# A local-attention and gated-FFN kernel: one weight row tile moved to another DMA queue, a new hand-written order, and six output tiles stored in halves

## The chip, the cores and the metric

The kernel runs on one core of one Trainium2 chip. The metric is the device time of one execution in microseconds (us); the time of a kernel is the median over its runs. Five engines work side by side, each through its own queue of instructions and strictly in that queue's order: TensorE (PE, with its weight load PEld), VectorE (DVE), ScalarE (ACT), GpSimd (POOL) and SyncE (SP). SP only issues DMA transfers here; ACT and POOL issue a few as well.

## The reference, cut to what matters

With S = 2048 tokens, D = 448, 16 heads of 28, F = 1792, all in bf16:

```
xn = (x - mean(x)) / sqrt(var(x) + 1e-5)
q, k, v = split(xn @ wqkv)                       # wqkv 448 x 1344
idx = pos - 2 * [0..7]                           # window of 8, dilation 2
attn = softmax(where(idx >= 0, q . k[idx] / sqrt(28), -1e9))
s = concat_heads(attn . v[idx]) @ wo
g = silu(gelu(xn @ w1 + b1) @ w2 + b2)           # 448 -> 1792 -> 448
out = x + s * g
```

## The kernel before, in words

Tokens are taken in 16 row tiles of 128, the even tokens first (tiles 0 to 7) and then the odd ones, so that a dilated window becomes a contiguous one. Tiles form four chunks of four (TPC = 4). Each tile is loaded, its mean and variance taken (`stats`, DVE, L429 and L433), its rstd found (`rstds`: a square root on ACT, L441, and a reciprocal on DVE, L444, for tiles 0 to 3; POOL, L450 and L451, for the others), normalized (L469) and transposed to xnT. For tiles 0 to 3 the transposes run on PE (L504; tile 3 in half-row form, L488) and DVE or ACT copies them out (L318, L320); for the others a DMA transposes. Contraction length 448 is three full row tiles of 128 rows and one of 64 rows; the 64-row products of two partners run in pairs, one in each half of the PE array, so that two of them take the time of one (`together`). Nearly all products go through `product` (L521): q, k and v, the FFN's first and second product, and wo. Attention runs in 9 visits, each of scores (L800), exp (L809), mask (L815) and values times weights (L833); the results are turned by DVE (L845, L870), scaled and moved (L853, L864, L866). v goes through a scratch in HBM (v_hbm) and comes back in windows (L375). The last two steps are `gated`: s*g (L944 or L946), the addition of x (L951) and the store (L958). The last output tile, 15, is cut into a part of 352 columns (LAST) and one of 96.

PE has no real work until x and the weights have landed. Until then it multiplies a constant of ones: the *fill* matmuls (L333), nine of 512 columns and then some of 128. [...]

The order of all work is written out by hand. Every piece of work is a task of `_Plan`, numbered in the order in which the code adds it. `ORDER` is a list of task numbers; `run` places the tasks one after the other in that list's order (a negative number puts the task on its second engine), and `emit` issues them in it. The costs and `tail` numbers of a task serve the planner's own clock; they become no instruction. Their one effect is a limit of 8.0 on the fills: a fill that the planner's clock would put later is left out. So the list is the order in each engine's queue.

Numbers that matter below: tasks 1 to 48 are the fills; the first DMA issues are x of tile 0 (on ACT) and x of tile 1, the three row tiles of wqkv (`w_in`, 336 KB each), x of tiles 2 and 3 and the 64-row tails of wqkv (`w_in3`, two DMAs of 112 KB) on SP, then w1 (`w`) and x of tiles 4 to 7. b1 comes through POOL's queue, in rows, and is turned by one PE transpose (L1033).

Of the kernel before, what the change touches and what calls it, by code (L numbers as in the profile page):

```python
# [66 lines left out]
]  # L67
LAST = 352
TWICE = ()
# [126 lines left out]
def kernel(  # L196
# [12 lines left out]
    nc = tc.nc  # L209
    P = 128  # L210
# [162 lines left out]
    def dma_sb(dst, src, deps, take=(), late=False):  # L373
        def fn(k):
            (nc.gpsimd if k.on == "POOL" else nc.sync).dma_start(dst(k), src())  # L375
        a = plan.add("SP" if late else ("SP", "POOL"), 0.45 if late else (0.45, 0.6), fn, deps, take=take)
        return a, plan.add("DMA", 0.45, lambda _: None, [a], tail=2.2)
# [23 lines left out]
    load_x(0, 1, "ACT", tail=1.45)  # L401
# [3 lines left out]
    def load_w(kt, tail):  # L405
        t_w.append([dma("SP", w_in[:, kt, :], A_wqkv[kt * P:(kt + 1) * P, :], 336, rate=262.0, tail=tail, share=1)])

    load_w(0, 0.85)
    load_w(1, 1.4)
    load_x(2, 1, "SP", tail=1.45)  # L410
    load_w(2, 1.45)
    load_x(3, 1, "SP", tail=1.4)
    tails = A_wqkv[KF:D, :].rearrange("p (w d) -> p w d", d=D)
    t_w.append([dma("SP", w_in3[:64], tails[:, 0:3:2, :], 112, issue=0.6, rate=262.0, tail=1.3),
                dma("SP", w_in3[64:], tails[:, 1:3, :], 112, issue=0.6, rate=262.0, tail=1.3)])
# [3 lines left out]
    t_b1r.tail = 5.0  # L419


    plan.add("ACT", 0.2, lambda _: nc.scalar.activation(sd[:, :1], eps_t[:], ACT.Sqrt), [t_eps], table=("sqrt",))
# [15 lines left out]
    def rstds(t0, n):  # L438
# [8 lines left out]
        else:  # L447
# [4 lines left out]
            b = plan.add("POOL", 0.7 + 0.25 * n, f, [t_st[t] for t in range(t0, t0 + n)] + [t_eps])  # L452
# [387 lines left out]
    def output_of(b, po):  # L840
# [6 lines left out]
        for a in (1, 0):  # L847
            def f6(k, a=a):
                nc.vector.reciprocal(buf(p_rd, k)[:], buf(p_dt, d[a])[:].rearrange("p (b c) -> p b c", c=32)[:, :, DH])
            r = plan.add("DVE", 0.25, f6, [d[a]], take=(p_rd,))  # L850

            def f7(k, a=a, r=r):
                nc.vector.tensor_tensor(out=turned_in(d[a]).rearrange("p l b c -> p (l b) c")[:, :, :DH],  # L853
                                        in0=buf(p_dt, d[a])[:].rearrange("p (b c) -> p b c", c=32)[:, :, :DH],
                                        in1=buf(p_rd, r)[:].unsqueeze(2).to_broadcast((P, H, DH)), op=ALU.mult)
            m.insert(0, plan.add("DVE", dve(D), f7, [r], give=((p_rd, r, 0),)))
        for a in range(2):
            moved = []
# [12 lines left out]
            o = plan.add("DVE", dve(512), f9, moved + turned_out[a][-1:], give=((p_dt, d[a], 0),))  # L871
# [178 lines left out]
    for g in range(G):  # L1050
        k, at = 3 + g // 2, (112 * (g % 2) + 84) + 12 * (g // 2)
        t_wo.append(dma("POOL", wo[32 * g:32 * g + 28, :k, :], A_wo[112 * g:112 * g + 28 * k, :].rearrange("(l c) d -> c l d", l=k), 25 * k, [t_w2[1][0]]))
        t_wo.append(dma("POOL", wo[32 * g + 28:32 * g + 32, :k, :], A_wo[at:at + 4 * k, :].rearrange("(l c) d -> c l d", l=k), 4 * k, [t_w2[1][0]]))
# [71 lines left out]
```

## Time and profile before

| what | value |
|---|---|
| time, median of 3 runs | 150.65 us (149.36, 150.65, 151.14) |
| time of the profiled execution | 149.33 us |
| span of its trace, granted PE clock | 147.6 us, 0.996 |
| PE busy | 143.1 us, 97% of the span, 2265 matmuls |
| DVE, ACT, POOL busy | 108.4, 100.2, 32.2 us |
| DMA moved | 19.47 MB in 38054 packets |

The profiled execution is as fast as the fastest of the three runs. Its span covers the recorded instructions; 149.33 - 147.6 = 1.7 us of its time lie outside. A row of the timeline gives the start, how long the group lasted from its first start to its last end, engine and line, what was written from what, the shape, and in brackets how long the engine idled before and who ended that. Matmuls are pipelined: the next starts before the last one ends, so the step from start to start is shorter than the duration of one.

### The profile page before, as it was taken

The numbers are of one execution on the slowest core, as the hardware profiler recorded it, in microseconds if no ns is written. First come the engines' busy times: TensorE is split into PE (matmuls) and PEld (weight loads), VectorE is DVE, ScalarE is ACT, GpSimd is POOL, SyncE is SP. The second block draws the span as 40 slices with busy tenths as digits, with TensorE's granted clock in tenths as the row PEclk, the third lists the DMA queues.
The fourth block names the chain that finished last, engine by engine and source line by source line (L and its number), as shares of the span: only waits on it lengthen the run. The fifth ranks groups of instructions, "written<-read, shape, count | busy, mean of one in ns | idle before, by whom it ended". The sixth has DMA issues, their size and how long they took to land.

```text
span 147.6 us, 5461 instructions
## 1 busy us (share of the span) xinstructions
PE 143.1 (97%) x2265; PEld 78.7 (53%) x2265; DVE 108.4 (73%) x273; ACT 100.2 (68%) x185; POOL 32.2 (22%) x89
## 2 busy tenths in 40 slices
PE   7999999999999999999999999999999999999990
PEld 2545555555556665555557654545565454555560
DVE  2784850547636467977797998977978979997772
ACT  3257777778678657859729887999686597921620
POOL 4122255103061002961122000041011004401000
PEclk9999999999999999999999999999999999999998
DMA  4999964999999930799772796560422000011112
GB/s 150 323 313 330 124 178 77 231 177 296 260 133 204 145 65 14 208 185 172 172 156 71 107 154 154 159 138 4 136 73 69 4 0 4 0 59 39 62 62 64
DMA packets 38054, 19.47 MB, mean 132 GB/s; under 512 B 24999, under 2 KB 37258, under 8 KB 38030
## 3 DMA queue, kind: packets, MB, share of 16 engines
q1 hardware_dynamic: 36958, 17.42, 55.7%
q0 software_dynamic: 784, 1.57, 4.5%
q8 instruction: 17, 0.28, 0.8%
q10 hardware_dynamic: 288, 0.14, 0.3%
q14 instruction: 7, 0.06, 0.1%
HBM read 9.42 MB, written 3.94 MB: 90 GB/s over the span
## 4 chain that ended last, share of the span: by engine, by line
PE 93%; DVE 2%; DMA 2%; issue 0%; DVEq 0%
PE bank L521 83%; PE bank L755 3%; PE bank L800 3%; PE bank L833 2%; DMA x_sb<-in_A_x_dram 2%; DVE sg L944 1%; DVE st L429 1%; PE bank L504 1%; PE bank L932 0%; PE bank L333 0%; DVE o L951 0%; DVE xn L469 0%; PE bank L753 0%; DVE mv L433 0%; PE bank L488 0%
## 5 line engine op out<-in xcount | busy, mean ns | idle before, releaser
L521 PE MATMUL bank<-xnT,w 64*128 64x512 bf16 (+1 forms) x428 | 46.1, 377 | 0.0
L521 PE MATMUL bank<-w,h 64*128 64x448 bf16 (+1 forms) x440 | 41.5, 350 | 0.0
L705 ACT ACTIVATE h<-bank,b 128x512 bf16<-128x512 f32 x56 | 35.2, 686 | 7.3 <-PE bank L521 7.0
L521 PE MATMUL bank<-w_in,xnT 64*128 64x448 bf16 (+2 forms) x342 | 36.6, 350 | 0.0
L521 PEld LDWEIGHTS <-w 64*128 64x128 bf16 (+1 forms) x428 | 20.3, 94 | 20.1
L521 PEld LDWEIGHTS <-h 64*128 64x128 bf16 (+1 forms) x440 | 19.5, 93 | 14.7
L521 PEld LDWEIGHTS <-xnT 64*128 64x128 bf16 (+2 forms) x342 | 16.8, 94 | 13.5 <-issue 0.6
L809 ACT ACTIVATE E<-bank 128x456 bf16<-128x456 f32 (+1 forms) x36 | 17.1, 555 | 6.0 <-PE bank L800 6.0
L318 ACT CAST qk_tok<-bank 128x448 bf16<-128x448 f32 x28 | 14.2, 532 | 7.2 <-PE bank L521 5.4
L429 DVE BATCH_NORM_STATS2 st<-x_sb 128x6 f32<-128x448 bf16 x16 | 9.6, 611 | 9.7 <-DMA x_sb<-in_A_x_dram 9.6
L866 POOL COPY wide<-wide 64x64 bf16<-64x64 bf16 x23 | 7.0, 318 | 40.7 <-DVE wide L853 20.3
L845 DVE STREAM_TRANSPOSE wide<-bank 128x512 f32<-128x512 f32 x18 | 12.3, 691 | 2.9 <-PE bank L833 2.1
L870 DVE STREAM_TRANSPOSE oT<-wide 128x512 bf16<-128x512 bf16 x18 | 12.2, 692 | 1.5 <-ACT wide L864 0.6
L815 DVE TENSOR_TENSOR E<-E,m_gen 128x456 bf16<-128x456 bf16 (+1 forms) x32 | 11.9, 386 | 1.8 <-ACT E L809 1.8
L521 PE MATMUL bank<-wo,oT 64*128 64x448 bf16 x98 | 11.5, 349 | 0.0
L853 DVE TENSOR_TENSOR wide<-wide,rd 128x448 bf16<-128x448 f32 x18 | 11.1, 622 | 0.3
L767 DVE TENSOR_TENSOR wide<-bank,b 128x448 f32<-128x448 f32 x15 | 9.0, 614 | 2.8 <-PE bank L521 2.8
L685 ACT ACTIVATE kd<-qkT,head 128x1024 bf16<-128x1024 bf16 x8 | 8.9, 1160 | 2.6 <-DMA qkT<-qk_tok 2.6
L469 DVE TENSOR_SCALAR xn<-x_sb,mv,rstd 128x448 bf16<-128x448 bf16 x16 | 6.0, 393 | 4.5 <-POOL rstd L451 4.4
L833 PEld LDWEIGHTS <-v 64*32 64x32 bf16 x576 | 7.0, 91 | 3.6 <-issue 3.1
L946 DVE SCALAR_TENSOR_TENSOR sg<-bank,g 128x448 bf16<-128x448 f32 x12 | 7.1, 611 | 2.2 <-PE bank L521 2.2
L779 ACT ACTIVATE wide<-wide 128x448 f32<-128x448 f32 x12 | 6.8, 578 | 2.6 <-DVE wide L767 2.6
(77 smaller groups left out, 136.8 us busy)
## 6 DMA issues: line engine op xcount, KB each, us to landing
v<-v_hbm SPq DMA_DIRECT2D x14, 128.0 KB, 2.8
out_dram<-o SPq DMA_DIRECT2D x15, 112.0 KB, 1.8
v_hbm<-v_tok SPq DMA_DIRECT2D x12, 128.0 KB, 3.0
w<-in_B_w_dram SPq DMA_DIRECT2D x2, 672.0 KB, 6.6
w_in<-in_A_wqkv_dram SPq DMA_DIRECT2D x3, 336.0 KB, 4.9
x_sb<-in_A_x_dram SPq DMA_DIRECT2D x4, 224.0 KB, 2.7
w<-in_B_w_dram SPq DMA_DIRECT2D x2, 448.0 KB, 4.4
w<-in_B_w_dram SPq DMA_DIRECT2D x2, 336.0 KB, 5.8
```

Source lines behind the costliest of these rows:

```text
L318: nc.scalar.copy(o, i)
L429: nc.vector.bn_stats(out=buf(p_st, k)[:], in_=x_sb[:, t, :])
L521: return nc.tensor.matmul(ps[rows, :n], lhsT[:, rows], rhs, start=start, stop=stop)
L685: nc.scalar.activation(dst, src, ACT.Copy, scale=head[:, a:a + 1])
L705: nc.scalar.activation(buf(p_h, own, i)[:], buf(p_b, own, i)[:], ACT.Gelu_apprx_tanh, bias=b1[:, mt:mt + 1])
L767: nc.vector.tensor_tensor(out=buf(p_y, k)[:, :n], in0=buf(p_b, own, i)[:, :n], in1=b2[:, cs], op=ALU.add)
L809: nc.scalar.activation(buf(p_E, k)[:, :8 * n], buf(p_b, a, at + i)[:, :8 * n], ACT.Exp, scale=SCALE)
L815: nc.vector.tensor_tensor(out=E, in0=E, in1=m[:, :, :, :n].rearrange("p i g q -> p (i g) q"), op=ALU.mult)
L833: nc.tensor.matmul(banks[a][32 * g:32 * g + 32, c0:c0 + n], buf(*v_at[b])[r, s, 2 * g + h, :], buf(p_E, exps[2 * h + s // 2])[r, c1:c1 + n ...
L845: nc.vector.transpose(buf(p_dt, k)[:], buf(p_b, po, a)[:])
L853: nc.vector.tensor_tensor(out=turned_in(d[a]).rearrange("p l b c -> p (l b) c")[:, :, :DH], in0=buf(p_dt, d[a])[:].rearrange("p (b c) -> p ...
L870: nc.vector.transpose(oT[:, a::2, q:q + 256], turned_in(d[a]).rearrange("p l b c -> p l (b c)"))
```

## The change

It has five parts.

1. `load_w` takes an engine, and the second row tile of wqkv (rows 128 to 255) is issued by ACT, right behind x of tile 0. On SP it is gone from between the first row tile and x of tile 2.
2. The whole list `ORDER` is another one. 24 fills are issued instead of 16: 20 ahead of the first transposes instead of 12, then 3 and 1 instead of 4. The transpose of b1 comes ahead of the first product. The store of zeros ahead of v in its scratch leaves the head of SP's queue. At the end, the addition of x for the 352-column part of tile 15 goes to POOL and its store to ACT's queue.
3. `TWICE` names tiles 5 to 10: each is stored by two DMAs of 224 columns instead of one of 448.
4. The square-root activation on a constant (`t_root`, L422) writes the last column of `sd` instead of the first, and POOL's rstd tasks depend on it.
5. `moved` is one list for both halves of a visit: the last DVE transpose of either half waits for all copies so far.

The other numbers changed are the planner's costs and tails.

```diff
 ORDER = [
-    64, 1, 59, 54, 56, 55, 57, 2, 3, 4, 5, 6, 7, 49, 53, 52, 126, 50, 58, 82, 83, 86, 87, 88, 8, 9, 10, 11, 12, 66,
...
+    60, 64, 82, 66, 1, 83, 53, 52, 58, 49, 2, 50, 68, 70, 56, 51, 55, 3, 72, 4, 74, 5, 76, 6, 78, 7, 86, 80, 8, 87,
...
-TWICE = ()
+TWICE = (5, 6, 7, 8, 9, 10)
...
-    def load_w(kt, tail):
-        t_w.append([dma("SP", w_in[:, kt, :], A_wqkv[kt * P:(kt + 1) * P, :], 336, rate=262.0, tail=tail, share=1)])
-
-    load_w(0, 0.85)
-    load_w(1, 1.4)
-    load_x(2, 1, "SP", tail=1.45)
...
+    def load_w(kt, tail, eng="SP"):
+        t_w.append([dma(eng, w_in[:, kt, :], A_wqkv[kt * P:(kt + 1) * P, :], 336, rate=262.0, tail=tail, share=1)])
+
+    load_w(0, 1.8)
+    load_w(1, 1.2, "ACT")
+    load_x(2, 1, "SP", tail=1.5)
...
-    plan.add("ACT", 0.2, lambda _: nc.scalar.activation(sd[:, :1], eps_t[:], ACT.Sqrt), [t_eps], table=("sqrt",))
...
+    t_root = plan.add("ACT", 0.2, lambda _: nc.scalar.activation(sd[:, NT - 1:], eps_t[:], ACT.Sqrt), [t_eps], table=("sqrt",))
...
-            b = plan.add("POOL", 0.7 + 0.25 * n, f, [t_st[t] for t in range(t0, t0 + n)] + [t_eps])
+            b = plan.add("POOL", 0.7 + 0.25 * n, f, [t_st[t] for t in range(t0, t0 + n)] + [t_eps, t_root])
...
+        moved = []
         for a in range(2):
-            moved = []
             for x in range(2):
...
-            o = plan.add("DVE", dve(512), f9, moved + turned_out[a][-1:], give=((p_dt, d[a], 0),))
+            o = plan.add("DVE", dve(512), f9, list(moved) + turned_out[a][-1:], give=((p_dt, d[a], 0),))
```

Three places of the order follow. The names are the program's, with the number of a buffer behind them.

The first place is SP's queue at the start of the program. `x_sb` is x, `w_in` a row tile of wqkv, `w_in_65` its 64-row tails, `w_66` is w1. Before:

```order
L360 DMA x_sb<-in_A_x_dram 128x448
L360 DMA w_in<-in_A_wqkv_dram 128x1344 x2
L360 DMA x_sb<-in_A_x_dram 128x448
L360 DMA w_in<-in_A_wqkv_dram 128x1344
L360 DMA x_sb<-in_A_x_dram 128x448
L360 DMA w_in_65<-in_A_wqkv_dram 64x2x448
L360 DMA w_in_65<-in_A_wqkv_dram 64x896
```

and ACT's queue at the same place, after the change (`sd` is the square root, `bank` a PSUM bank):

```order
L360 DMA x_sb<-in_A_x_dram 128x448
L360 DMA w_in<-in_A_wqkv_dram 128x1344
L441 ACT_TABLE_LOAD
L441 ACTIVATE sd<-mv,eps_t 128x1
L422 ACTIVATE sd<-eps_t 128x1
L441 ACTIVATE sd<-mv,eps_t 128x1
L318 COPY xnT<-bank_162 128x2x128
```

One of SP's two loads in its second row is now ACT's second row; everything behind it on SP is one issue earlier.

The second place is PE where the first 64-row products with `w_in_65` come, after the full row tiles. Before:

```order
L521 MATMUL bank_165<-w_in,xnT 128x448
L521 LDWEIGHTS xnT
L521 MATMUL bank_166<-w_in,xnT 128x448
L521 LDWEIGHTS xnT
L521 MATMUL bank_164<-w_in_65,xnT 128x448
L521 LDWEIGHTS xnT
L521 MATMUL bank_166<-w_in_65,xnT 128x448
```

and after:

```order
L504 MATMUL bank_167<-ident,xn_93 128x128
L521 LDWEIGHTS xnT
L521 MATMUL bank_163<-w_in,xnT 128x448
L521 LDWEIGHTS xnT
L521 MATMUL bank_164<-w_in,xnT 128x448
L521 LDWEIGHTS xnT
L521 MATMUL bank_161<-w_in,xnT 128x448
L521 LDWEIGHTS xnT
L521 MATMUL bank_168<-w_in_65,xnT 128x448
L521 LDWEIGHTS xnT
L521 MATMUL bank_166<-w_in_65,xnT 128x448
```

Between the first product and the first 64-row product stood 14 full-row products, a transpose of b1 and 4 transposes (of tile 1); now 18 full-row products and 8 transposes (of tiles 1 and 2) stand there.

The third place is the end of the program on DVE. `g` is the gate, `sg` is s*g, `o` the output tile. Before:

```order
L944 TENSOR_TENSOR sg_119<-bank_167,g_118 128x352
L951 TENSOR_TENSOR o_123<-x_sb,sg_119 128x352
L944 TENSOR_TENSOR sg_120<-bank_163,g_116 128x448
L951 TENSOR_TENSOR o_122<-x_sb,sg_120 128x448
L944 TENSOR_TENSOR sg_119<-bank_165,g_117 128x96
L951 TENSOR_TENSOR o_121<-x_sb,sg_119 128x96
```

and after, where POOL's last row is the addition that DVE lost, `L951 TENSOR_TENSOR o_122<-x_sb,sg_119 128x352`:

```order
L944 TENSOR_TENSOR sg_119<-bank_167,g_115 128x352
L944 TENSOR_TENSOR sg_120<-bank_168,g_116 128x448
L951 TENSOR_TENSOR o_121<-x_sb,sg_120 128x448
L944 TENSOR_TENSOR sg_119<-bank_163,g_118 128x96
L951 TENSOR_TENSOR o_123<-x_sb,sg_119 128x96
```

The 352-column addition has left DVE; the multiplication that feeds it still stands first.

More of the change, by code (lines that the diff above doesn't have):

```diff
@@ L375, in fn @@
             (nc.gpsimd if k.on == "POOL" else nc.sync).dma_start(dst(k), src())
-        a = plan.add("SP" if late else ("SP", "POOL"), 0.45 if late else (0.45, 0.6), fn, deps, take=take)
+        a = plan.add("SP" if late else ("SP", "POOL"), 0.52 if late else (0.52, 0.65), fn, deps, take=take)
         return a, plan.add("DMA", 0.45, lambda _: None, [a], tail=2.2)
@@ L398, in ktiles @@
         return ap.rearrange("(k p) c -> p k c", p=P)
-    load_x(0, 1, "ACT", tail=1.45)
+    load_x(0, 1, "ACT", tail=1.65)
     load_x(1, 1, "SP", tail=1.2)
     t_w = []
-    def load_w(kt, tail):
-        t_w.append([dma("SP", w_in[:, kt, :], A_wqkv[kt * P:(kt + 1) * P, :], 336, rate=262.0, tail=tail, share=1)])
-    load_w(0, 0.85)
-    load_w(1, 1.4)
-    load_x(2, 1, "SP", tail=1.45)
-    load_w(2, 1.45)
-    load_x(3, 1, "SP", tail=1.4)
+    def load_w(kt, tail, eng="SP"):
[3 more added lines that the diff above has]
+    load_x(2, 1, "SP", tail=1.5)
+    load_w(2, 1.55)
+    load_x(3, 1, "SP", tail=1.6)
     tails = A_wqkv[KF:D, :].rearrange("p (w d) -> p w d", d=D)
-    t_w.append([dma("SP", w_in3[:64], tails[:, 0:3:2, :], 112, issue=0.6, rate=262.0, tail=1.3),
-                dma("SP", w_in3[64:], tails[:, 1:3, :], 112, issue=0.6, rate=262.0, tail=1.3)])
+    t_w.append([dma("SP", w_in3[:64], tails[:, 0:3:2, :], 112, issue=0.6, rate=262.0, tail=1.7),
+                dma("SP", w_in3[64:], tails[:, 1:3, :], 112, issue=0.6, rate=262.0, tail=1.7)])
     t_b1z = plan.add("POOL", 0.1, memset("gpsimd", b1r, 0.0), [t_on])
     t_b1r = dma("POOL", b1r[:NMT], B_b1.rearrange("(m f) -> m f", f=P), 4, [t_b1z])
-    t_b1r.tail = 5.0
-    plan.add("ACT", 0.2, lambda _: nc.scalar.activation(sd[:, :1], eps_t[:], ACT.Sqrt), [t_eps], table=("sqrt",))
+    t_b1r.tail = 3.2
+    t_root = plan.add("ACT", 0.2, lambda _: nc.scalar.activation(sd[:, NT - 1:], eps_t[:], ACT.Sqrt), [t_eps], table=("sqrt",))
     t_st = {}
@@ L1051 @@
         k, at = 3 + g // 2, (112 * (g % 2) + 84) + 12 * (g // 2)
-        t_wo.append(dma("POOL", wo[32 * g:32 * g + 28, :k, :], A_wo[112 * g:112 * g + 28 * k, :].rearrange("(l c) d -> c l d", l=k), 25 * k, [t_w2[1][0]]))
-        t_wo.append(dma("POOL", wo[32 * g + 28:32 * g + 32, :k, :], A_wo[at:at + 4 * k, :].rearrange("(l c) d -> c l d", l=k), 4 * k, [t_w2[1][0]]))
+        t_wo.append(dma("POOL", wo[32 * g:32 * g + 28, :k, :], A_wo[112 * g:112 * g + 28 * k, :].rearrange("(l c) d -> c l d", l=k), 25 * k, [t_w2[1][0]], issue=0.62))
+        t_wo.append(dma("POOL", wo[32 * g + 28:32 * g + 32, :k, :], A_wo[at:at + 4 * k, :].rearrange("(l c) d -> c l d", l=k), 4 * k, [t_w2[1][0]], issue=0.62))
     t_wo.append(plan.add("POOL", 0.9, lambda _: nc.gpsimd.tensor_copy(wo[:64, 3, :], wo[64:, 3, :]), t_wo[4:]))
```

82 rows, old and new, of the table ORDER are left out of this document.

## The prediction

> **What bounds the kernel now.** I read the page's busy shares first, then the windows, cut where the kind of work changes.
>
> ```profile
> PE 143.1 (97%) x2265; PEld 78.7 (53%) x2265; DVE 108.4 (73%) x273; ACT 100.2 (68%) x185; POOL 32.2 (22%) x89
> ```
>
> ```profile
> 0.00:5.40 5.40, 4.32 (x12) 1.61 (x12) 2.71 (x17) 1.58 (x2) 1.62 (x8) 1.00 0.63 198
> 5.40:11.30 5.90, 5.86 (x50) 3.46 (x51) 4.28 (x17) 2.71 (x8) 1.51 (x8) 1.00 1.05 322
> 11.30:45.00 33.70, 33.70 (x332) 17.96 (x330) 18.06 (x59) 25.93 (x45) 10.40 (x29) 1.00 1.04 200
> 45.00:137.00 92.00, 92.00 (x1822) 51.20 (x1818) 77.00 (x171) 66.45 (x126) 18.31 (x43) 1.00 0.48 98
> 137.00:143.00 6.00, 6.00 (x38) 3.54 (x37) 4.43 (x10) 3.21 (x5) 0.34 (x2) 1.00 0.23 77
> 143.00:147.60 4.60, 1.25 (x22) 0.92 (x19) 1.96 (x6) 0.30 (x2) 0.00 (x0) 0.86 0.18 52
> ```
>
> In a windows row stand the stretch, its length, and the busy time of PE, PEld, DVE, ACT and POOL with counts; then clock, DMA share and GB/s. From 11.3 to 143.0, 131.7 us, PE is busy for the whole of each stretch. No better order of the other engines can take anything there beyond what is hidden inside pipelined matmuls. The change leaves PE's real work as it is, so it can act at three places: the 11.3 us ahead of that stretch, the 4.6 us behind it, and on how an execution with late DMAs differs from this one.
>
> PE's own waits say how little is to be had. Beside the program's start there is one of more than a trace of time:
>
> ```profile
> PE bank L504 <- DVE xn L469: 0.3, 1, 0.3
> ```
>
> That is the idle time ahead of the first transposes.
>
> **The start.** PE's timeline, with the two other engines' rows that set its times:
>
> ```profile
> 0.84 4.32 PE L333 MATMUL bank<-const-bfloat16-1.0 128*128 128x512 bf16 x12 [0.84 <-PEq L1109]
> 5.45 0.39 PE L504 MATMUL bank<-ident,xn 128*128 128x128 bf16 x2 [0.28 <-DVE xn L469]
> 5.63 0.63 PE L333 MATMUL bank<-const-bfloat16-1.0 128*128 128x128 bf16 x4
> 6.06 0.42 PE L504 MATMUL bank<-ident,xn 128*128 128x128 bf16 x2
> 6.27 0.78 PE L521 MATMUL bank<-w_in,xnT 128*128 128x448 bf16 x3
> ...
> 7.00 0.35 PE L521 MATMUL bank<-w_in,xnT 128*128 128x448 bf16 x1
> ...
> 7.25 0.54 PE L521 MATMUL bank<-w_in,xnT 128*128 128x448 bf16 x2
> ...
> 7.74 2.70 PE L521 MATMUL bank<-w_in,xnT 128*128 128x448 bf16 x13
> 10.27 0.28 PE L504 MATMUL bank<-ident,xn 128*128 128x128 bf16 x2
> 10.57 0.28 PE L504 MATMUL bank<-ident,xn 128*128 128x128 bf16 x2
> 10.78 0.36 PE L521 MATMUL bank<-w_in,xnT 64*128 64x448 bf16 x2
> ```
>
> ```profile
> 3.54 0.63 DVE L429 BATCH_NORM_STATS2 st<-x_sb 128x6 f32<-128x448 bf16 x1 [1.73 <-DMA x_sb<-in_A_x_dram]
> 4.99 0.40 DVE L469 TENSOR_SCALAR xn<-x_sb,mv,rstd 128x448 bf16<-128x448 bf16 x1
> ```
>
> The chain is x of tile 0 landed (3.54), statistics, xn done (4.99 + 0.40 = 5.39), first transposes 5.45, first product 6.27.
>
> *Fills, 20 instead of 12.* The step of a short fill comes from the second fill row: 0.63 for four, of which I take 0.31 for the last (a pair of them, 0.42, is one step and one duration), so (0.63 - 0.31) / 3 = 0.107. The first row gives the long ones: 4.32 = 9 steps + 2 x 0.107 + 0.31, so 0.42 each. Twenty fills keep PE until 0.84 + 9 x 0.42 + 11 x 0.107 = 5.80, where xn is ready at 5.39: the first transposes start 0.35 later. Behind them stand 9 short rows before the first product (3 fills, b1's transpose, 2 transposes, 1 fill, and the first pair) where 8 took 6.27 - 5.45 = 0.82. At the old step that makes 5.80 + 0.92 = 6.72. But PE gets faster about here: two transposes take 0.42 at 6.06 and 0.28 at 10.27, so a step falls from 0.107 to about half of that, 0.055. If the last rows run at the fast step it is 6.55. I take 6.62, so **+0.35** (bounds 0, if x is so late that xn comes after the fills, and +0.45). b1's transpose no longer stands among the products, where it takes a fast step: **-0.06**.
>
> *w_in3.* The row at 7.74 holds 8 full-row products, one 64-row pair (two matmuls in one slot) and 3 more: 12 slots. A product alone lasts 0.35 (7.00), two last 0.54 (7.25), so the step is 0.19. At that it would last 11 x 0.19 + 0.35 = 2.44; it lasts 2.70. Two changes between full and 64-row work lie in it. One alone costs 10.78 - (10.57 + 2 x 0.055) = 0.10, so 0.06 is left for the pair's wait on `w_in3`. These are its second half and the x and weights ahead of it:
>
> ```profile
> L360 SPq DMA_DIRECT2D w_in<-in_A_wqkv_dram x1: 593/593/593, 4.4 to 4.4; - x1
> ...
> DMA to landing us min/median/max: 5.0/5.0/5.0
> ```
>
> It landed at 9.4, when PE stood before it since 9.35. The wait was at its edge, and any lateness of that transfer went into the time one to one. Afterwards 18 products and 8 transposes stand ahead: 6.62 + 0.05 (one step more for the switch of speed) + 18 x 0.19 + 8 x 0.055 = 10.5, and the issue is a row earlier. The wait goes, **-0.06**, and a slack of 1.1 us takes its place. Next late would be x of tile 2: its transposes now stand ahead of these products.
>
> *w_in row tile 1 on ACT.*
>
> ```profile
> 1.26 0.89 SPq L360 DMA_DIRECT2D w_in<-in_A_wqkv_dram  x2
> ```
>
> ```profile
> L360 SPq DMA_DIRECT2D w_in<-in_A_wqkv_dram x1: 412/412/412, 1.3 to 1.3; - x1
> ...
> DMA to landing us min/median/max: 4.3/4.3/4.3
> ```
>
> Two issues in 0.89: each load behind on SP goes out 0.45 earlier. ACT has nothing to do before the first square root, 4.3 us or later (statistics end at 3.54 + 0.63 and an aggregate), so its extra issue is covered by the wait for x. What can be lost is row tile 0: issued at 1.26, it landed at 1.3 + 4.3 = 5.6, with PE wanting it at 6.27 and now at 6.62. If its rival's 336 KB all go ahead of it, at the 322 GB/s of the second window it lands 1.04 later, 6.6, just in time; at the first window's 198 GB/s, 1.7 later, 7.3. Both were in flight together before, 0.45 apart, so I take 0 (bounds 0 and +0.7). [...]
>
> **The body.** One pair of rows of the chain shows the only stall that I find inside: a visit of scores takes 0.43 as a rule, and once 0.57.
>
> ```profile
> 59.19 0.43 PE bank L800 x32
> 67.54 0.57 PE bank L800 x32
> ```
>
> A new order makes it likely that this 0.14 goes and possible that others come: I take **-0.1**, bounds -0.2 and +0.5 (three such stalls). The six extra stores lie on SP, an engine that mostly waits for the work it is to store:
>
> ```profile
> SPq L958 <- DVE o L951: 20.2, 7, 6.1
> ```
>
> 6 x 0.33 (an issue, row below) = 2.0 us against 20 us of waiting for these additions alone: 0. Where the shared `moved` list makes a DVE transpose wait for copies of its visit's other half, DVE is covered by its own idle 27%: 0. The constant square root is moved by a column: 0.
>
> **The end.** The timeline of the last stretch, POOL's nearest row, and the stores:
>
> ```profile
> 142.79 0.52 DVE L944 TENSOR_TENSOR sg<-bank,g 128x352 bf16<-128x352 f32 x1 [0.73 <-PE bank L932]
> 143.35 0.34 DVE L951 TENSOR_TENSOR o<-x_sb,sg 128x352 bf16<-128x352 bf16 x1
> 143.61 0.62 DVE L944 TENSOR_TENSOR sg<-bank,g 128x448 bf16<-128x448 f32 x1
> 143.72 1.29 SPq L958 DMA_DIRECT2D out_dram<-o  x2
> ...
> 144.85 0.21 DVE L951 TENSOR_TENSOR o<-x_sb,sg 128x96 bf16<-128x96 bf16 x1
> 145.10 0.35 ACTq L958 DMA_DIRECT2D out_dram<-o  x1
> ```
>
> ```profile
> L1054 POOL COPY wo<-wo 64x448 bf16<-64x448 bf16 x1 | 0.8, 806 | 5.5 <-PE bank L521 5.5
> ```
>
> ```profile
> out_dram<-o SPq DMA_DIRECT2D x15, 112.0 KB, 1.8
> ...
> out_dram<-o SPq DMA_DIRECT2D x1, 88.0 KB, 2.5
> ...
> out_dram<-o ACTq DMA_DIRECT2D x1, 24.0 KB, 1.6
> ```
>
> Before, the last store goes out at 145.10 and lands 1.6 later, 146.7. DVE's chain loses one addition, but the multiplication behind it is 0.26 later only (143.35 to 143.61), and its last addition still waits for the 96 columns from PE: I expect 0.1 less, 146.6. POOL's addition is the new end. It starts at 142.79 + 0.52 + 0.05 = 143.35. POOL's copy of 448 columns took 0.806; an addition reads twice as much. Bounds: 352/448 of the copy, 0.63, and twice that, 1.27; I take 0.9, nearer the copy, since the columns are fewer and the written elements the same in kind. The store goes out at 143.35 + 0.9 + 0.05 = 144.3 and, with 2.5 to landing, lands at 146.8: **+0.13** against 146.7 (bounds -0.1 and +0.5). It decides from an addition of 0.77 up. [...] No row here shows a POOL addition of bf16.
>
> The halves end in rows of 448 bytes. [...]
>
> **The sum.** 0.35 - 0.06 - 0.06 - 0.1 + 0.13 = +0.26 on an execution like the profiled one: 149.33 + 0.26 = 149.6. The median of the runs is 1.32 above the profiled execution, whose transfers landed at the edge (w_in3) or early. I take it that the runs around the median are those with later DMAs. The slacks then decide: x of tile 0 may be 0.35 late for nothing, w_in3 1.1. I let them take about half of the 1.32, so the median stands about 0.6 above the sum: **150.2**, 0.3% below 150.65.
>
> **The rivals.** About 1%, 1.5 us, is what a measurement of this kernel can tell from no change: faster is below 149.1, slower above 152.2.
>
> *All lateness is absorbed, or PE is fast earlier.* Then the median is the sum, 149.6. Beyond that the fills close PE's 0.28 gap. If the fast step began as the fills end, they would not hold the transposes up (-0.35), and 8 rows would go at 0.055 instead of 0.107 (-0.4): 148.8. For it speaks that PE is then never idle between 0.84 and the products. Against it, the fast step came at about 6.4 in spite of the gap. [...]
>
> *Row tile 0 lands later, and nothing is absorbed.* PE waits at its first product as soon as that landing passes 6.62. With the median's 1.32 on the sum it is 150.9, with half of the 0.7 above 151.2: slower than before. For it speaks that two queues now issue 336 KB each at one moment, at a DMA share of 0.63 rising to 1.05; against it, the 0.45 between them before.
>
> *A new hold-up in the body.* PE's order now stands in other places against the copies on POOL and the windows of v. A single wait of some length on each of three or four visits, 0.5 each, gives 151.9; with unabsorbed lateness 152.5. Against it speaks that DVE, ACT and POOL have 27%, 32% and 78% idle.
>
> **How the numbers follow.** Forecast 0.45 (its own range 149.5 to 151), all absorbed or fast early 0.25 (148.6 to 149.6), row tile 0 late 0.18 (150.9 to 151.8), hold-up 0.12 (151.7 to 153). Half of the second case and a little of the first lie below 149.1: faster 0.14. Slower is the hold-up and a little of the third: 0.14. The rest, 0.72, is the same. The range leaves out the hold-up's upper part and the second case's last bit: 148.8 to 151.8.
>
> **What would show it.** In the profile after: 20 fills, first transposes near 5.8 without idle time, first product at 6.5 to 6.7; no wait at the first 64-row products, near 10.5; PE busy throughout from 11.5 to 143; the 352-column addition on POOL at 0.65 to 1.25 and a last landing set by its store. It would be wrong if PE waited for `w_in` at the first product, if the chain held POOL or v in the body, or if the runs scattered by more than 1.8 us as they do now.

## The result and the profile after

| | median | lowest to highest | runs |
|---|---|---|---|
| before | 150.55 us | 148.79 to 151.94 | 21 |
| after | 149.18 us | 148.82 to 150.48 | 21 |

The ratio of after to before is 0.9941, with a 95% interval of 0.9916 to 0.9965. The change makes the kernel faster by about 0.6%, 0.9 us. (The two medians lie 1.37 apart; I go by the ratio.) The fastest runs are alike, at 148.8; the long ones have become rare: 15 of the 21 took more than 150 us before, 2 of the 21 after. So the question is what varied from run to run before, and hardly does now. In the experiments below, runs more than 1.5% above the fastest of the same kernel count in no ratio.

The profiled execution of the changed kernel took 150.48 us, the slowest of its 21 runs, with a span of 148.7. It shows where the new order still gives time away, and must be read with that in mind. Busy time, then windows, cut as before but for the end:

```profile
PE 142.8 (96%) x2273; PEld 75.7 (51%) x2273; DVE 108.3 (73%) x272; ACT 102.2 (69%) x190; POOL 29.2 (20%) x83
```

```profile
0.00:5.40 5.40, 4.21 (x21) 1.94 (x22) 2.37 (x14) 1.67 (x3) 1.71 (x9) 1.00 0.64 207
5.40:11.30 5.90, 5.90 (x57) 3.36 (x57) 4.31 (x16) 3.28 (x10) 0.90 (x4) 1.00 1.07 328
11.30:45.00 33.70, 33.70 (x337) 15.76 (x330) 17.10 (x52) 24.25 (x43) 11.91 (x33) 1.00 0.88 187
45.00:137.00 92.00, 90.52 (x1804) 49.72 (x1802) 76.79 (x174) 70.44 (x131) 13.46 (x36) 1.00 0.55 102
```

Between 5.4 and 45 us PE issued 7 and 5 matmuls more than before in the same time. From 45 to 137 it issued 18 fewer and was idle for 1.48 us (92.00 - 90.52). PE's waits name both holes of that stretch, and its timeline places them:

```profile
PE bank L521 <- DMA xnT<-xn: 1.2, 1, 1.2
PE bank L333 <- PEq L1109: 0.9, 1, 0.9
PE bank L504 <- DVE xn L469: 0.3, 1, 0.3
PE bank L521 <- ACT E L809: 0.2, 1, 0.2
```

```profile
59.28 0.93 PE L521 MATMUL bank<-w_in,xnT 64*128 64x448 bf16 x8 [1.24 <-DMA xnT<-xn]
```

```profile
106.58 0.72 PE L521 MATMUL bank<-wo,oT 64*128 64x448 bf16 x5 [0.25 <-ACT E L809]
```

The first, 1.24 us for a DMA transpose of x, is in this profile alone of all of the new order. Take it away, and this run is at 149.24, close to the median. The second is in all six profiles of the new order and in that of the hybrid with the new body. It belongs to the order.

To compare whole profiles I added up, for every matmul but the fills, the time that it takes from start to start when PE is fast and waits for nothing (0.189 us for 448 columns, half of that for one of a 64-row pair), and subtracted the sum from the clock. What remains is the time that PE has lost so far. Changes between full and partial arrays are in it, and nearly alike in all: up to 12 us the old order has two more of them than the new one, about 0.1 each. In us, at four marks, and in the last column the span less the start of the last matmul (of the runs, the experiments follow below):

```
                                 12 us   60 us   75 us  143 us  end
before                            6.39    6.77    7.60   10.10  3.6
after                             5.75    7.59    8.45   11.32  3.4
e1_few_fills                      6.04    6.47    7.17   10.05  3.4
e2_before_20_fills                6.36    6.74    8.78   11.11  3.9
e3_before_w1_act                  6.45    6.83    8.06   10.38  3.8
e4_w1_on_sp                       6.00    6.53    7.23   10.02  3.7
e5_v_buffers                      6.80    7.09    7.89   10.24  3.4
e6_new_start_old_body             5.85    6.75    9.14   11.39  4.0
e7_old_start_new_body             6.88    7.59    8.30   11.10  4.6
e8_no_halves                      6.23    6.66    7.37   10.22  4.2
e9_new_start_old_body_v_buffers   5.97    6.88    8.72   11.31  3.7
e10_after_v_buffers               5.83    6.26    7.04    9.87  3.4
e11_tail_on_dve                   5.88    6.31    7.01    9.80  3.7
e12_e9_halves                     6.07    6.98    8.41   10.84  4.1
```

Three things stand in it. At 12 us the new start has lost 5.75 to 6.23, the old one 6.36 to 6.88. From 60 to 75 us the new body loses 0.70 to 0.86; the old one 0.83, 1.23, 2.04 and 2.39 in its four profiles without further buffers. From 75 to 143 us the new body loses 2.8 to 2.9 (2.79 to 2.88), the old one 2.25 to 2.6.

### The profile page after: what moved, and what is told of

Its sections match the earlier page's. It is cut to its first block, busy times and chain, and to the rows that moved or that the text cites. A ratio compares the mean times of both kernels' runs of the same rounds, so it can differ in the third digit from the quotient of the medians.

```text
span 148.7 us, 5486 instructions
## 1 busy us (share of the span) xinstructions
PE 142.8 (96%) x2273; PEld 75.7 (51%) x2273; DVE 108.3 (73%) x272; ACT 102.2 (69%) x190; POOL 29.2 (20%) x83
## 4 chain that ended last, share of the span: by engine, by line
PE 81%; DMA 13%; DVE 3%; issue 1%; ACT 0%; DVEq 0%; ACTq 0%
PE bank L521 71%; DMA xnT<-xn 11%; PE bank L755 3%; PE bank L833 2%; PE bank L800 2%; DMA x_sb<-in_A_x_dram 2%; PE bank L932 1%; DVE st L429 1%; DVE sg L944 1%; PE bank L504 1%; ACT E L809 0%; DVE kd L687 0%; DVE o L951 0%; DVE xn L469 0%; PE bank L333 0%
## 5 line engine op out<-in xcount | busy, mean ns | idle before, releaser
L521 PEld LDWEIGHTS <-w 64*128 64x128 bf16 (+1 forms) x428 | 19.0, 94 | 21.3
L521 PEld LDWEIGHTS <-xnT 64*128 64x128 bf16 (+2 forms) x342 | 15.7, 94 | 16.2 <-DMA xnT<-xn 1.7
L318 ACT CAST qk_tok<-bank 128x448 bf16<-128x448 f32 x26 | 13.3, 537 | 7.3 <-PE bank L521 6.7
L866 POOL COPY wide<-wide 64x64 bf16<-64x64 bf16 x20 | 5.4, 278 | 43.6 <-PE bank L521 16.2
L521 PE MATMUL bank<-wo,oT 64*128 64x448 bf16 x98 | 11.5, 349 | 0.2 <-ACT E L809 0.2
L320 DVE CAST v_tok<-bank 128x448 bf16<-128x448 f32 x4 | 2.5, 616 | 9.0 <-PE bank L521 9.0
```

The costliest lines, as they stand in the source:

```text
L318: nc.scalar.copy(o, i)
L521: return nc.tensor.matmul(ps[rows, :n], lhsT[:, rows], rhs, start=start, stop=stop)
```

## The theories

*Fills:* the 20 fills keep PE busy until x is there, so its fast step comes earlier. *Slack, or start:* weights and x may land later without PE noticing. *Store:* the old body hangs, at 65 to 67 us, on how late the stores of v to HBM land. The last came out of the table after the first four runs; the expectation of those calls it the body theory. This is ACT in the kernel before, at the place where the prediction had seen only a visit of scores last 0.57 us instead of 0.43:

```profile
65.14 0.97 ACT L318 CAST v_tok<-bank 128x448 bf16<-128x448 f32 x2 [0.36 <-DMA v_hbm<-v_tok]
66.72 0.97 ACT L318 CAST v_tok<-bank 128x448 bf16<-128x448 f32 x2 [0.62 <-DMA v_hbm<-v_tok]
```

There are four buffers `v_tok`. ACT's casts for tiles 8 to 11 write into those of tiles 4 to 7, and have to wait until the stores of these, issued from 59.3 to 61.0, have read them. Behind the casts on ACT's queue stand an evacuation and the exp of the visit; behind the banks that they free stands PE. Of the four stores POOL's queue issues the last two, and the last lands 5.6 us later, at 66.7:

```profile
L375 POOL DMA_DIRECT2D v_hbm<-v_tok x2: 603/702/802, 60.4 to 61.0; - x2
```

The new order keeps away from this. In the changed kernel's trace two of the tiles 4 to 7 are cast at 29.0 and 30.6 already, and their stores are issued by 51.7. The other two are cast at 57.3 and 58.2, and SP alone issues their stores, which have landed by 62.6:

```profile
59.41 1.00 SPq L375 DMA_DIRECT2D v_hbm<-v_tok  x2
```

So ACT's casts into these buffers, which begin at 65.2, wait for PE and for ACT's own work, and for no store:

```profile
65.21 0.53 ACT L318 CAST v_tok<-bank 128x448 bf16<-128x448 f32 x1 [0.56 <-PE bank L521]
66.48 0.97 ACT L318 CAST v_tok<-bank 128x448 bf16<-128x448 f32 x2 [0.30 <-ACT qk_tok L318]
```

## The experiments

All ratios are to the kernel before, which ran beside each on the same chip, with 95% intervals.

**e1, fewer fills in the changed kernel.**

```diff
-        t_warm = plan.add("PE", 0.427 if i < 9 else 0.107, fn, [t_warm], take=(p_b,), limit=8.0)
+        t_warm = plan.add("PE", 0.427 if i < 9 else 0.107, None if 12 <= i < 20 else fn, [t_warm], take=(p_b,), limit=8.0)
```

> The changed kernel with 12 fills ahead of the first transposes as before, instead of 20 (the other 12 of the 24 stay). Fills theory (the gain comes from PE being kept busy until x is there, so that its fast step begins earlier): most of the gain goes, the ratio to before comes out near 1.000 (0.997 to 1.003), and the first products show the slow step in the profile. Slack theory (the gain comes from weights and x that may land later): nothing changes, ratio 0.994 (0.991 to 0.997). Body theory (the gain comes from the order after the first 11 us): 0.994 as well.

Measured 0.9927 (0.9897 to 0.9957), median 149.23 over 8 runs. The gain is all there: the fills theory falls.

**e2, 20 fills in the kernel before.** Tasks 13 to 20 are put behind task 12 in the old `ORDER`; the four fills between the transposes become tasks 21 to 24.

> The kernel before with 20 fills ahead of its first transposes, all else as it was. Fills theory: most of the gain, ratio 0.994 to 0.997. Slack theory: at best 0, at worst the 0.35 us of the prediction's first term, ratio 1.000 to 1.003. Body theory: the same, 1.000 to 1.003.

Measured 0.9988 (0.9960 to 1.0016). No effect that can be told from none. Its profile, span 148.9, is where the store theory came from. Waits of PE, then ACT and PE at the place of the rows above:

```profile
PE bank L521 <- ACT v_tok L318: 1.1, 1, 1.1
```

```profile
66.72 1.84 ACT L318 CAST v_tok<-bank 128x448 bf16<-128x448 f32 x4 [1.97 <-DMA v_hbm<-v_tok]
```

```profile
67.31 1.50 PE L521 MATMUL bank<-w,h 64*128 64x448 bf16 x14 [1.11 <-ACT v_tok L318]
```

The same four casts, with the same order ahead of them, start 1.6 us later than in the profile before, and PE waits 1.11 us for them.

**e3, row tile 1 of wqkv on ACT in the kernel before.** `load_w(1, 1.4, "ACT")`, and task 70 right behind 64 in the old `ORDER`.

> The kernel before with the second row tile of wqkv issued by ACT behind x of tile 0, all else as it was; the transfers behind it on SP go out 0.45 us earlier. Slack theory: PE's order still stands at the edge of w_in3, but that lands up to 0.45 earlier, so about a half of the gain, ratio 0.996 to 0.998. Fills theory and body theory: 1.000 (0.998 to 1.002). If the two loads disturb each other: above 1.002, with PE waiting for w_in at its first product.

Measured 0.9968 (0.9937 to 0.9998), the size that the slack theory expected. But in its profile PE had lost 6.45 us at 12 us, not less than before (6.39), and 1.23 from 60 to 75. So this profile shows no gain in the sum at the start, and the interval nearly reaches 1. The slack itself can be seen in it. The second half of `w_in3`, issued at 3.9 instead of 4.4, landed at 8.9, and PE came to the products with it at 9.46 and did not wait. In the four profiles with the old order's start and both loads on SP it landed between 9.4 and 9.9, and PE waited each time (0.07 to 0.75 us, see below). Against that, the fast step came latest of all here, at 6.6. Whether the waits avoided make up the 0.3% is not shown.

**e4, that row tile back on SP in the changed kernel.** `load_w(1, 1.2, "SP")`.

> The changed kernel with that row tile issued by SP as before, so that all behind it go out 0.45 us later; the new order keeps its 1.1 us of slack ahead of the first 64-row products. Slack theory: the slack covers most of the 0.45, so ratio 0.994 to 0.997. Fills theory and body theory: 0.994 (0.991 to 0.996).

Measured 0.9905 (0.9873 to 0.9938), median 149.07 over 6 runs. The load on ACT is not needed for the gain; PE's loss at 12 us is 6.00, within what the profiles with it show (5.75 to 6.23).

**e5, four more buffers for v in the kernel before.** The order is untouched. Tiles 8 to 11 are cast into the last 512 columns of each row of `oT`, which the attention writes much later.

```diff
+    v_more = [oT[:, j, 12 * P:16 * P].rearrange("p (a x c) -> p a x c", a=2, c=32) for j in range(4)]
...
-            v = v_tok[t % len(v_tok)]
+            v = v_more[t - 8] if 8 <= t < 12 else v_tok[t % 4]
```

> The kernel before with four more buffers for v, so that ACT's casts of v at 65 to 67 us no longer wait for the stores of the four tiles before; the order is that of before. Store theory (the gain is above all that the new order no longer hangs on how late those stores land): the profile shows no wait of ACT on v_hbm<-v_tok there, PE's loss against its ideal between 60 and 75 us falls from 0.8 to 2.0 to about 0.7, and the ratio to before is 0.993 to 0.997 with a smaller scatter. Start theory (the gain is made in the first 12 us): 1.000 (0.998 to 1.002).

Measured 0.9911 (0.9876 to 0.9946), median 149.13, lowest 148.66, highest 149.33 over 6 runs. One wait taken out of the old order is worth as much as the whole change. The runs lie closer together too, as far as 6 of them can tell. ACT at that place no longer waits for a store:

```profile
65.26 1.84 ACT L318 CAST oT<-bank 128x448 bf16<-128x448 f32 x4 [0.15 <-PE bank L521]
```

**e6, new start and old body.** The first 256 entries of the new `ORDER`, then the old one without them; stores undivided, the zero store of v and the list `moved` as before the change.

> The new order up to about 25 us (24 fills, row tile 1 on ACT), and all tasks behind it in the old order; stores undivided, the zero store of v where it was before. Start theory: most of the gain, 0.993 to 0.996. Store theory: only the 0.3 to 0.6 us that the start shows in the profiles, 0.996 to 0.999, and the wait for v stores at 65 to 67 us stays with its scatter.

Measured 1.0088 (1.0051 to 1.0125): slower than either, which no theory expected. PE's longest wait in it, and the row of ACT behind that:

```profile
PE bank L521 <- ACT v_tok L318: 1.4, 1, 1.4
```

```profile
67.06 1.84 ACT L318 CAST v_tok<-bank 128x448 bf16<-128x448 f32 x4 [2.39 <-DMA v_hbm<-v_tok]
```

The start is the new one (5.85 lost at 12 us). From 60 to 75 us it loses 2.39. The store theory has the place right and the size wrong: here the casts waited 2.39 us for a store of v.

**e7, old start and new body.** The first 256 entries of the old `ORDER`, then the new one; row tile 1 on SP, stores undivided.

> The old order up to about 25 us (16 fills, row tile 1 on SP) and all tasks behind it in the new order, stores undivided. Store theory: more than half of the gain, 0.993 to 0.997, small scatter. Start theory: 0.998 to 1.002.

Measured 1.0045 (1.0015 to 1.0075), also slower. The new body has no wait for stores of v (0.71 from 60 to 75 us). But the start loses 1.0 us between the first product and 12 us, most of it (0.75) here:

```profile
9.46 1.46 PE L521 MATMUL bank<-w_in,xnT 64*128 64x448 bf16 x5 [0.25 <-DMA w_in<-in_A_wqkv_dram]
```

That is the edge of `w_in3`, with the transfer late. It also has the longest end of all, 4.6 us (more under e8). The two hybrids show that the gains of start and body do not simply add. That each part of an order has been set for what the other does to the queues is my reading; no run tests it alone.

**e8, the changed kernel with undivided stores.** `TWICE = ()`, and the order without the second halves' tasks.

> The changed kernel with all stores undivided, everything else as changed. All theories: nothing, 0.990 to 0.996 as the changed kernel, since these stores lie where nothing waits for them. If the halves free buffers of the output sooner in a way that matters, PE or DVE show a new wait between 100 and 143 us and it is 0.2 us or more slower than the changed kernel.

Measured 0.9965 (0.9940 to 0.9990), median 149.98, all 12 runs from 149.58 to 150.53. The other kernels with the new order and halves lie at 0.9905 to 0.9941, so this one is 0.2 to 0.6% above them. The expectation was nothing. None of them ran beside it, and the interval overlaps that of the change, so the loss is likely and not certain. In its profile the end is 4.2 us long, and 4.6 in e7, whose stores are undivided too; the five profiles of the new order with halves have 3.4 to 3.7. The start is 0.2 to 0.5 worse in e8 as well (the fills, below). At its end DVE's last multiplication of 448 columns waits 0.61 us, where it waits 0.23 after the change. The view names PE, which had been done for some 0.4 us by then, so what it waited for is not known.

**e9, e6 with the further buffers for v.** Both edits together.

> The kernel of the run with the new start and the old body, with the four more buffers for v, stores undivided. Store theory: the 1.4 us wait that this hybrid showed for ACT's casts of v goes, and what stays is the better start; PE's loss against its ideal is about 6.0 at 12 us and rises by 0.8 from 60 to 75 us and by 2.3 from 75 to 143 us; ratio 0.987 to 0.992, which would beat both kernels. A rival that the hybrid is slow for another reason (its junction, or the ends of its stores): 1.000 or above.

Measured 1.0051 (1.0018 to 1.0084): a miss. The wait for stores of v has gone as expected, and another has taken its place, on ACT and behind it on PE:

```profile
70.59 0.53 ACT L318 CAST qk_tok<-bank 128x448 bf16<-128x448 f32 x1 [1.61 <-DMA qkT<-qk_tok]
```

```profile
71.17 1.18 PE L521 MATMUL bank<-w_in,xnT 64*128 64x448 bf16 x6 [0.36 <-ACT qk_tok L318]
```

It is the same mechanism on the next ring of buffers: `qk_tok` is cast anew when its DMA transpose has read it. The joint of the two orders, the rival that the expectation named, costs something as well: from 12 to 60 us the three kernels with the new start and the old body lose 0.9 us (e6, e9, e12), the kernel before 0.4. A part of it is this wait, which neither parent has:

```profile
35.94 1.69 PE L521 MATMUL bank<-xnT,w 64*128 64x512 bf16 x14 [0.17 <-POOLq L569]
```

**e10, the further buffers for v in the changed kernel.**

> The changed kernel with the four more buffers for v. Store theory: the new order has no wait left there, so nothing: 0.990 to 0.996 as the changed kernel. If the buffers help by something else (the same memory written elsewhere, other semaphores), it gains as much as the kernel before did: 0.983 to 0.988.

Measured 0.9910 (0.9877 to 0.9943), median 148.94, from 148.81 to 149.43 over 7 runs. Its interval overlaps that of the change (0.9916 to 0.9965): the buffers add little or nothing where the order keeps away from the stores, against 0.9% in the old order. If the change and the buffers took away different losses, the two gains would make about 0.985 together, which lies below the interval. So the two take away much the same loss.

**e11, the 352-column addition on DVE and its store on SP.** Two signs in the new `ORDER`: task 1047 instead of -1048, 1048 instead of -1049.

> The changed kernel with the addition of x for the 352 columns back on DVE and its store back on SP. The prediction's third term had POOL's addition 0.13 us dear: then 0.1 us faster than the changed kernel, inside its scatter, 0.990 to 0.996. If DVE is the end of the chain instead: the 96-column store goes out 0.3 us later and it is 0.2 to 0.3 us slower.

Measured 0.9934 (0.9911 to 0.9957), as the change. Its end, on DVE and ACT:

```profile
144.81 0.21 DVE L951 TENSOR_TENSOR o<-x_sb,sg 128x96 bf16<-128x96 bf16 x1 [0.29 <-DMA out_dram<-o]
145.05 0.34 ACTq L958 DMA_DIRECT2D out_dram<-o  x1
```

The last addition waits for a buffer of `o` that an earlier store still reads, so where the 352 columns are added does not set the end in this run.

**e12, e9 with halves.** Only SP's queue differs from e9.

> The first kernel of this call with the six output tiles stored in halves; only SP's queue differs. If the halves are worth what the run without them lost (0.3%): 0.2% to 0.4% below the first kernel of this call. If that was scatter or the end of that program alone: the same within 0.2%.

Measured 1.0044 (1.0012 to 1.0077), against 1.0051 of e9: the same, within these intervals. The halves show no worth in the old body. Its profile has one cost of the new start that no term of the prediction has: the transpose of b1, now ahead of the first product, waited for b1 to land.

```profile
PE bank L1033 <- DMA E<-in_B_b_dram: 0.3, 1, 0.3
```

## Why the prediction was right, and where it was not

The range (148.8 to 151.8) held the time, and the direction was right. The forecast, 150.2, was 1.0 us above the median, 0.3% of gain against 0.6% by the ratio; the rival that all lateness is absorbed gave 149.6 and stood nearer. That the range held is in part luck. The wait for the stores of v is in no term of the sum, the hold-up in the body, a rival with a chance of 0.12, is there in part, and the +0.35 of the fills did not come; these errors partly cancel. Some of the signs that the prediction named failed: the first transposes came at 5.33 after an idle 0.33 us, not near 5.8 without, the first product at 6.01, not from 6.5, and PE was not busy throughout from 11.5 to 143.

*Where it was right.* Nothing could be had from the busy stretch but stalls inside it, and the scatter of the runs, not the profiled execution, was what the change could act on. The `w_in3` edge is real. From the first product to 12 us the old start lost 0.34, 0.40, 0.47, 0.84 and 1.00 in its five profiles; the new one less than 0.1 in all nine. Not all of this is the wait: the old start also has the two further changes between full and 64-row work, and in some profiles its first products go at the slow step. The wait is how far the second of the first two 64-row matmuls starts behind the place that the steps give it, read from the traces: 0.07 in the kernel before, where the prediction had 0.06, 0.25 in e2, 0.52 in e5 and 0.75 in e7. Each time that matmul started 0.04 after the second half of `w_in3` had landed; in e3, where the transfer was early, there was no wait. So the mechanism was right, and the size in the profiled execution too. In e5 two matmuls that else share a slot, and last 0.36 together, take 0.73, because the transfer issued at 4.4 lands at 9.7:

```profile
9.37 0.73 PE L521 MATMUL bank<-w_in,xnT 64*128 64x448 bf16 x2
```

```profile
L360 SPq DMA_DIRECT2D w_in<-in_A_wqkv_dram x1: 592/592/592, 4.4 to 4.4; - x1
...
DMA to landing us min/median/max: 5.3/5.3/5.3
```

*The fills, +0.35.* Mis-sized: 0 in most profiles. With 20 fills the first transposes came at 5.33 to 5.59 in eight of nine profiles, with 12 at 5.43 to 5.51 in all five. They delayed the transposes where PE was slow until then, above all in e8, whose timeline has the first transposes at 5.82 with no wait ahead of them, where the prediction had 5.80:

```profile
0.86 5.13 PE L333 MATMUL bank<-const-bfloat16-1.0 128*128 128x512 bf16 x20 [0.86 <-PEq L1109]
5.82 0.28 PE L504 MATMUL bank<-ident,xn 128*128 128x128 bf16 x2
```

In the changed kernel's own profile the same 20 took 4.15, and xn set the time:

```profile
0.86 4.15 PE L333 MATMUL bank<-const-bfloat16-1.0 128*128 128x512 bf16 x20 [0.86 <-PEq L1109]
5.33 0.29 PE L504 MATMUL bank<-ident,xn 128*128 128x128 bf16 x2 [0.33 <-DVE xn L469]
...
6.01 0.74 PE L521 MATMUL bank<-w_in,xnT 128*128 128x448 bf16 x3
```

Whether an unbroken row of fills makes the fast step come sooner, as the fills theory and the rival of an early fast step had it, is not shown: the step came between 3.8 and 5.8 us in the nine profiles with 20 fills, between 3.8 and 6.6 in the five with 12, and e1 kept the gain with 12.

*The body, -0.1.* This is the step that failed. The 0.14 us at 67.5 was found, and priced from the one execution in which it happened to be small. I did not ask what the engine named there was waiting for in turn. The rows of ACT quoted above were in the trace before: 0.36 and 0.62 us of waiting for a DMA store, on a queue that PE waits for. That wait on a landing was a sample, not a constant: in three profiles of the old order with its own buffers PE lost 0.83, 1.23 and 2.04 from 60 to 75 us, where 0.70 to 0.86 is what the stretch costs without it. That seems to be more of the scatter than the start: with the wait removed and the old start kept (e5), 6 runs spread over 0.7 us, while the 22 that count of the kernel before, run beside it, spread over 2.1. Six runs are few, and in e5's own profile the start still waited 0.52 us for `w_in3`. The prediction laid the 1.32 us of lateness to the start and let half of it pass.

*A new hold-up, 0.5 a piece.* There is one: the row at 106.58 above. The products of wo there take banks that ACT's exp has not yet freed. In PE's loss it makes a step of about 0.5 us at 105, the difference of the two bodies from 75 to 143. So the change gained some 0.6 at the start (the means of the new and the old profiles at 12 us), lost 0.5 at 105, and removed the wait for stores, which was worth 0.9% (e5). That e5 and the change come out alike fits this: start and hold-up nearly cancel. It is a sum over profiles of single executions, not a measurement of each.

*The end, +0.13.* The addition was priced about right, and nothing came of it in time, because the landing of its store was mis-sized. POOL's addition took 0.85 (0.9 was taken, 0.63 to 1.27 the bounds):

```profile
144.01 0.52 DVE L944 TENSOR_TENSOR sg<-bank,g 128x352 bf16<-128x352 f32 x1 [1.12 <-PE bank L932]
144.68 0.85 POOL L951 TENSOR_TENSOR o<-x_sb,sg 128x352 bf16<-128x352 bf16 x1 [3.45 <-DVE sg L944]
...
145.55 1.06 ACTq L958 DMA_DIRECT2D out_dram<-o  x2
...
146.02 0.21 DVE L951 TENSOR_TENSOR o<-x_sb,sg 128x96 bf16<-128x96 bf16 x1
```

Its store is the first of ACT's two, and took 1.7 from issue to landing, not the 2.5 that the one of before had taken:

```profile
out_dram<-o ACTq DMA_DIRECT2D x1, 88.0 KB, 1.7
```

Issued at 145.55 it landed at 147.3, ahead of the 96-column store, issued from 146.26 on with 1.5 to landing, which ended the program. By the prediction's own sum an addition of more than 0.77 decides the end; with 1.7 in place of 2.5 it did not. With the addition on DVE (e11) the time was the same.

*The halves, 0.* Probably wrong in the new order, where e8 came out 0.2 to 0.6% above the others, and its end and that of e7 were longer by 0.5 to 1.2 us; right in the old body (e12), within the noise. The halves did not land later: after the change the twelve of 56 KB on SP landed 1.6 us after their issue, the nine undivided stores of 112 KB there 1.7 (medians). The expectation of e8 names a suspect, the buffers of the output: the last addition did wait for an output store in the new order, 0.29 us in e11 and 0.35 in e4. But these have halves; without them, in e8's trace, it was 0.15, so this wait did not grow. The cause stays open.

*The extra load on ACT.* Nothing, as taken: row tile 0 landed in time in all profiles with it (issued at 1.27 in the changed kernel's profile, landed 4.0 later, at 5.3, with the first product at 6.01), and e4 shows that the change does not need it.

## What to carry to other kernels

When runs scatter more than the profiled execution explains, look for every wait that ends with a DMA landing on a queue that the bound engine hangs on, however short it is in that one profile, and follow it back to its ring of buffers: one more set of buffers there, or an order that reuses them later, may be worth more than the stall shows (here 0.9% in e5, 1.3 us, for the visit of scores that lasted 0.14 us too long). The two orders of this case could not be cut and joined for their good parts: both joined ways came out slower than either. And a kernel that has got rid of one late landing should be profiled again for the next (in e9, 1.61 us of ACT's waiting for a transpose of `qk_tok`).

## What the runs showed of the hardware

PE's step falls to about half (from 0.107 to 0.056 us for 128 columns, from 0.427 to 0.220 for a fill of 512) at a moment that differs from execution to execution: in 14 profiles between 3.8 us (after, e5) and 6.6 us (e3), with the same first matmul at 0.8 to 0.9, so 2.9 to 5.8 us after it. With 20 fills it came by 5.8 in all nine profiles; with 12 at 3.8, by 5.4, and at about 6.1, 6.5 and 6.6. So the number of fills did not settle it, and the time did not follow it (e1, e2). The windows' column of granted clock reads 1.00 in the first stretch all the same. What sets the moment, no run shows.

From issue to landing the same transfer took 1.6 us more in one profile than in another, and in a second case 3.9. The stores of v, issued from 59.3 to 61.0 in both, let ACT's casts go at 65.1 in the profile before and at 66.7 in that of e2: the third of them took 4.6 us to land in the one and 6.2 in the other. Of these four stores the two issued by SP landed after 2.2 to 4.0 us, the two issued by POOL after 4.6 to 6.5, in the profiles before and of e2, e3 and e5; whether the queue does this or the later moment, no run shows. The transpose of x issued at 52.1 in the changed kernel's profile took 7.2 us to land, the same one in e10 (issued at 51.3) 3.3; the first is the one that PE waited 1.24 us for.
